# Cosine-weighted linear attention and a gated MLP on one core: load buffers shared by all batches but the second, and ten more zero matmuls in the opening

## The chip, the cores and the metric

One core of one Trainium2 chip. The metric is device time in microseconds (us) of one execution; several runs are given by their median. In the profile, PE is TensorE (matmul), PEld its weight load, DVE VectorE, ACT ScalarE, POOL GpSimd and SP SyncE; L259 is line 259 of the kernel file.

## What is computed

q, k and v have 8 batches, 8 heads, 576 positions and 64 values per head; the weights are 512 x 2048 and 2048 x 512.

```python
def phi(x, c, s):
    r = np.maximum(x, 0.0)
    return np.concatenate([r * c, r * s], axis=-1)   # cos and sin of pi/2 * pos / S
q_p, k_p = phi(q, cos_w, sin_w), phi(k, cos_w, sin_w)
kv = np.einsum('bhsf,bhsd->bhfd', k_p, v)
z = np.sum(k_p, axis=2)
num = np.einsum('bhsf,bhfd->bhsd', q_p, kv)
den = np.einsum('bhsf,bhf->bhs', q_p, z)[..., None] + 1e-06
x = (num / den)            # heads side by side: 4608 tokens x 512
h = x @ w_in
out = (h * np.cos(h)) @ w_out
```

## The kernel before

**Tiling.** A batch's 576 positions lie as 96 partitions of 6 positions (R = 6, L33). The 4608 tokens of the MLP are nine chunks of 512. Chunk c of the MLP and the attention of later batches are interleaved by hand: a chunk has 32 steps, 16 groups of the first product (M1, `m1_group`, L254: four matmuls, cosine on ScalarE, product g on VectorE) and 16 parts of the second (M2, `m2_part`, L272: four matmuls; every fourth part ends with a copy `ost` on ScalarE and stores to HBM from SP's queue). After each step, `run(c, s)` issues the attention pieces that `plan` has put there with `at(c, s, function, ...)` (L298). The order on each engine is the order of the program (`manual_schedule`, L382); the framework adds the waits, and a tile that takes a buffer over waits for the last reader of the tile before it, wherever in the program that reader stands.

**Attention pieces.** `load` (L83) is a DMA from POOL's queue that casts 32-bit inputs to 16-bit tiles k16, v16, q16. `scaled` (L100) applies the rectifier and the cosine or sine weight on VectorE, one position index i at a time (two instructions), giving kp and qp. `q_turn` (L120) transposes qp into X: on TensorE for batches 0 and 1, by a DMA transpose from SP's queue for the others (L125). `spread_v` (L159) copies v beside a column of ones (vz, whose ones are a memset on POOL, L163). `kv_head` (L171) multiplies kp and vz. `num_tile` and `normalise` (L200, L224) make the tile x of 128 tokens, which has three buffers (opool, L58). `x_turn` (L231) transposes x into XT, the input of M1: on TensorE for batches 0 and 1, by a DMA transpose from SP's queue for the others (L236).

**Where the pieces stand.** In chunk c of 1 and later: the tiles of batch c+1 at steps 16, 18, 20, 22, 24 (`plan_tiles`); for batch c+2 the q scaling and its transposes at steps 21, 23, ..., 31, v at 24, 26, 28, 30, the k scaling at 26, 28, 30 and, in chunk c+1, at 1, 3, 5 (`plan_ahead`, L349). Batch 2's q scaling ends at step 8 of chunk 1 (L342). Loads of batch 3 are issued at step 9 of chunk 1 (L345), of batch c+2 at step 1 of chunk c from chunk 2 on (L372), each as three DMAs by `loads` (L304). POOL's queue holds, in order, the loads and weight loads of the opening, the vz memsets and these loads.

**The load buffers.** lpool (L55) has two buffers for each tag, so batches take turns: 0, 2, 4, 6 in one, 1, 3, 5, 7 in the other.

**The opening** (L383 to L431): the loads are issued; TensorE multiplies a tile of zeros (`warm`, L407), 26 times 512 columns, before its first q transposes, which need qp of VectorE, which needs the q load. Then come the kp and v products of batch 0 (48 matmuls of 128 columns, L190), the first tiles, and M1 of chunk 0 in halves of 256 tokens.

Of the kernel before, what the change touches and what calls it, by code (L numbers as in the profile page):

```python
# [13 lines left out]
F16 = mybir.dt.float16  # L14
# [3 lines left out]
def kernel(  # L18
# [10 lines left out]
    B, H, S, D = q.shape  # L29
# [4 lines left out]
    PR = S // R  # L34
# [6 lines left out]
    RUN = R * D  # L41
# [10 lines left out]
    id_dr = nc.inline_tensor(np.eye(P, dtype=np.float16), name="id_const")  # L52

    cpool = ctx.enter_context(tc.tile_pool(name="cpool", bufs=1))
    lpool = ctx.enter_context(tc.tile_pool(name="lpool", bufs=2))  # L55
    apool = ctx.enter_context(tc.tile_pool(name="apool", bufs=2))
    gpool = ctx.enter_context(tc.tile_pool(name="gpool", bufs=2))
    opool = ctx.enter_context(tc.tile_pool(name="opool", bufs=3))  # L58
# [15 lines left out]
    st = {}  # L74

    def tiles_for(b):
        st[b] = dict(
            k16=lpool.tile([PR, H * RUN], F16, name="k16", tag="k16"),
            v16=lpool.tile([PR, H * RUN + D], F16, name="v16", tag="v16"),
            q16=lpool.tile([PR, H * RUN], F16, name="q16", tag="q16"),  # L80
        )

    def load(b, which, h0=0, h1=H, i0=0, i1=R):  # L83
        src = dict(k=k, v=v, q=q)[which]
        dst = st[b][which + "16"][:, 0:H * RUN]
        dst = dst.rearrange("p (h r) -> p h r", h=H)
        nc.gpsimd.dma_start(  # L87
            out=dst[:, h0:h1, i0 * D:i1 * D],
            in_=src[b].rearrange("h (p i) d -> p h (i d)", i=R)[:, h0:h1, i0 * D:i1 * D],
        )  # L90

    def load_w_in(g):
        sl = slice(g * CH, (g + 1) * CH)
        nc.gpsimd.dma_start(out=w_in_sb[:, :, sl], in_=w_in_v[:, :, sl])

    def load_w_out(g):
        sl = slice(g * 4, (g + 1) * 4)
        nc.gpsimd.dma_start(out=w_out_sb[:, sl, :], in_=w_out_v[:, sl, :])

    def scaled(b, which, i, h0=0, h1=H):  # L100
        s = st[b]
        if which + "p" not in s:
            s[which + "p"] = apool.tile([PR, R, H * F], F16, name=which + "p",
                                        tag=which + "p", bufs=1)
        dst = s[which + "p"][:, i].rearrange("p (h t d) -> p h t d", t=2, d=D)
        src = s[which + "16"][:, 0:H * RUN].rearrange("p (h i d) -> p h i d", i=R, d=D)
        for t in range(2):
            if b == 0 and (which == "k" and h0 == 4 and t == 1 or which == "q" and i == 4):
                nc.scalar.activation(
                    out=dst[:, h0:h1, t, :], in_=src[:, h0:h1, i, :], func=AF.Relu,  # L110
                    scale=CS[:, t, i:i + 1],
                )
                continue
            nc.vector.tensor_scalar(  # L114
                out=dst[:, h0:h1, t, :], in0=src[:, h0:h1, i, :],
                scalar1=0.0, scalar2=CS[:, t, i:i + 1],
                op0=ALU.max, op1=ALU.mult,
            )

    def q_turn(b, i, tag="m1"):  # L120
        s = st[b]
        if i == 0:
            s["X"] = apool.tile([P, H, S], F16, name="X", tag="X")
        if b >= 2:
            nc.sync.dma_start_transpose(  # L125
                out=s["X"][:, :, i * PR:(i + 1) * PR], in_=s["qp"][:, i],
            )
            return
        if b == 1:
            if i % 2 == 0:  # L130
                s["QT"] = psA.tile([P, 2, H, P], F16, name="QT", tag="att")
            QT = s["QT"][:, i % 2]
        elif i >= 4:
            QT = psA.tile([P, 2, H, P], F16, name="QT", tag="att")[:, 0]
        else:
            QT = psM.tile([P, H, P], F16, name="QT", tag=tag)
        for h in range(H):
            nc.tensor.matmul(  # L138
                QT[:, h, 0:PR], lhsT=s["qp"][:, i, h * F:(h + 1) * F], rhs=ID[0:PR, 0:PR],
                is_transpose=True,  # L140
            )
        if b == 1 and i % 2 == 0:
            return
        i0 = i - (b == 1)
        dst = s["X"][:, :, i0 * PR:(i + 1) * PR]
        if b == 1 and i > 1:
            nc.vector.tensor_copy(
                out=dst.rearrange("p h (a c) -> p a h c", a=2),
                in_=s["QT"][:, :, :, 0:PR],
            )  # L150
        elif b == 1:
            nc.scalar.activation(
                out=dst.rearrange("p h (a c) -> p a h c", a=2),
                in_=s["QT"][:, :, :, 0:PR], func=AF.Copy,
            )
        else:
            nc.scalar.activation(out=dst, in_=QT[:, :, 0:PR], func=AF.Copy)  # L157
# [13 lines left out]
    def kv_head(b, h):  # L171
        s = st[b]
        if h == 0 or (b == 0 and h == 4):
            s["KV"] = psA.tile([P, H, P], F32, name="KV", tag="att")
        if h == 0:
            s["kvz"] = apool.tile([P, H, D + 1], F16, name="kvz", tag="kvz")
        n = P if b == 0 else D + 1
        for i in range(R):
            if b > 0:
                nc.tensor.matmul(  # L180
                    s["KV"][:, h, 0:n], lhsT=s["kp"][:, i, h * F:(h + 1) * F],
                    rhs=s["vz"][:, h, i, 0:n], start=(i == 0), stop=(i == R - 1),
                )
                continue
            base = s["v16"][:, h * RUN + i * D: h * RUN + (i + 1) * D]
            vz = bass.AP(
                tensor=base.tensor, offset=base.offset,
                ap=[list(base.ap[0]), [H * RUN - h * RUN - i * D, 2], [1, D]],
            )
            nc.tensor.matmul(  # L190
                s["KV"][:, h], lhsT=s["kp"][:, i, h * F:(h + 1) * F], rhs=vz,
                start=(i == 0), stop=(i == R - 1),
            )
        if h % 4 == 3:
            nc.scalar.activation(  # L195
                out=s["kvz"][:, h - 3:h + 1], in_=s["KV"][:, h - 3:h + 1, 0:D + 1],
                func=AF.Copy,
            )
# [102 lines left out]
    HS = NJT  # L301
    M2S = NJT

    def loads(b, order="qkv"):  # L304
        tiles_for(b)
        for w in order:
            load(b, w)
# [70 lines left out]
    def run(c, s):  # L378
        for f, args in plan.pop((c, s), ()):
            f(*args)  # L380

    with tc.manual_schedule():  # L382
        nc.sync.dma_start(out=CS, in_=cs_dr.ap())  # L383
        nc.sync.dma_start(out=ID, in_=id_dr.ap())
        nc.vector.memset(WU, 0.0)
        nc.vector.memset(PIH, math.pi / 2.0)  # L386
        nc.scalar.activation(out=WS, in_=PIH, func=AF.Sin)
        tiles_for(0)
        load(0, "k", 0, 4)
        load(0, "k", 4, 8)  # L390
        load(0, "q", 0, H, 0, 4)
        for h in range(0, H, 2):
            load(0, "v", h, h + 2)
        nc.gpsimd.memset(st[0]["v16"][:, H * RUN:], 1.0)
        load_w_in(0)
        load(0, "q", 0, H, 4, R)
        for g in range(1, 4):
            load_w_in(g)
        load_w_out(0)
        load_w_out(1)  # L400
        loads(1, "kvq")
        load_w_out(2)
        load_w_out(3)
        loads(2, "kvq")
        W = psM.tile([P, CH], F32, name="W", tag="m2")

        def warm(n):  # L407
            for _ in range(n):
                nc.tensor.matmul(W, lhsT=WU[:, 0:P], rhs=WU, start=True, stop=True)  # L409

        warm(26)
        for h0 in (0, 4):
            for i in range(R):
                scaled(0, "k", i, h0, h0 + 4)
        for i in range(4):
            scaled(0, "q", i)
            if i < 2:
                q_turn(0, i)
        for h in range(8):
            kv_head(0, h)  # L420
        q_turn(0, 2, "m2")
        num_tile(0, 0)
        q_turn(0, 3)
        warm(1)
        num_tile(0, 1)
        warm(3)
        x_turn(0, 0)
        warm(2)
        scaled(0, "q", 4)
        x_turn(0, 1)  # L430
        num_tile(0, 2)  # L431
        for s in range(2 * HS):
            n = s // HS * (CH // 2)
            m1_group(0, s % HS, n, n + CH // 2)
            run(0, s)
        order = [(m, g) for p in (0, 2) for g in range(2) for m in (p, p + 1)]
        order += [(m, g) for m in range(NSUB) for g in range(2, 4)]
        for s, (m, g) in enumerate(order):
            m2_part(0, m, g)
            run(0, 2 * HS + s)  # L440
        for c in range(1, NCHUNK):
            for s in range(32):
                if s < NJT:
                    m1_group(c, s)
                else:
                    m2_part(c, (s - NJT) // 4, (s - NJT) % 4)
                run(c, s)
# [31 lines left out]
```

## Time and profile before

| what | us |
|---|---|
| median of 3 runs | 303.78 |
| the three runs | 304.11, 301.21, 303.78 |
| the profiled execution, its own time | 305.32 |
| its span, first to last instruction | 303.5 |
| TensorE busy | 292.9 |
| VectorE busy | 192.1 |
| ScalarE busy | 162.2 |

The profile is of one execution. Busy time is the union of an engine's instructions; idle time before a group is given with what ended it. The granted clock is the share of full speed that TensorE's throttle let through; a stretch's figure is a mean over it. The time to landing of a DMA goes from its issue to its completion. 1.8 us of the execution's own time lie outside its span.

### The profile page before, as it was taken

To read this page: it belongs to the slowest core of one execution; us is meant where nothing else is said; L and a number is where in the kernel's file an instruction comes from. 1 tells how busy PE (TensorE), PEld (TensorE's weight loads), DVE (VectorE), ACT (ScalarE), POOL (GpSimd) and SP (SyncE) were. 2 spreads that over 40 slices of the span, in tenths; PEclk is the share of its full clock that TensorE was granted. 3 is DMA by queue.
4 is the path that set the end of the run, shared out by engine and by line. 5 is a ranking of instruction groups with operands and counts; after the bars stand their busy time and mean duration, and the time that the engine had idled before them with its cause. 6 is when DMAs were issued, how large, how long until landed. Compare 5 with 4: busy or idle time off the path is not lost.

```text
span 303.5 us, 5549 instructions
## 1 busy us (share of the span) xinstructions
PE 292.9 (96%) x2088; PEld 155.1 (51%) x2088; DVE 192.1 (63%) x487; ACT 162.2 (53%) x262; POOL 29.2 (10%) x49
## 2 busy tenths in 40 slices
PE   8699999999999999999999999999999999999994
PEld 3578856554544554455445544554455444444441
DVE  2747896998579665966496739868675258107600
ACT  2559862577158715871577157725772177128521
POOL 8632103003000200020001100000000000000000
PEclk9789999999999999999999999999999999999998
DMA  7999999996996199729972997318621510121022
GB/s 103 191 206 205 205 205 202 229 191 102 193 192 153 33 181 232 137 59 170 212 163 63 160 188 183 81 38 147 141 49 38 129 53 2 35 69 38 0 69 69
DMA packets 73515, 38.81 MB, mean 128 GB/s; under 512 B 46352, under 2 KB 68880, under 8 KB 73488
## 3 DMA queue, kind: packets, MB, share of 16 engines
q0 software_dynamic: 23888, 18.35, 40.5%
q1 hardware_dynamic: 49600, 20.10, 33.7%
q8 instruction: 16, 0.26, 0.3%
q14 instruction: 11, 0.09, 0.1%
HBM read 36.74 MB, written 9.44 MB: 152 GB/s over the span
## 4 chain that ended last, share of the span: by engine, by line
PE 79%; DMA 9%; DVE 7%; ACT 2%; issue 1%; POOL 0%; ACTq 0%; DVEq 0%; POOLq 0%
PE M L259 35%; PE M L278 34%; DMA XT<-x 6%; PE KV L180 4%; DVE g L268 3%; PE NP L206 3%; DMA q<-in_q_dram 3%; DVE qp L114 2%; PE KV L190 2%; PE QT L138 1%; DVE kp L114 1%; ACT co L265 1%; DVE x L226 1%; PE XP L244 1%; POOL k L87 0%
## 5 line engine op out<-in xcount | busy, mean ns | idle before, releaser
L278 PE MATMUL M<-w_out_sb,g 128*128 128x512 f16 x576 | 132.3, 379 | 0.1
L259 PE MATMUL M<-XT,w_in_sb 128*128 128x512 f16 (+1 forms) x640 | 129.8, 358 | 1.7 <-DVE g L268 1.3
L268 DVE TENSOR_TENSOR g<-M,co 128x512 f16<-128x512 f32 (+1 forms) x160 | 98.6, 633 | 47.2 <-ACT co L265 47.0
L265 ACT ACTIVATE co<-M,PIH 128x512 f32<-128x512 f32 (+1 forms) x160 | 101.9, 646 | 28.7 <-PE M L259 25.3
L259 PEld LDWEIGHTS <-w_in_sb 128*128 128x128 f16 x640 | 61.2, 98 | 61.1 <-issue 2.5
L278 PEld LDWEIGHTS <-g 128*128 128x128 f16 x576 | 53.7, 98 | 58.7 <-issue 0.3
L285 ACT ACTIVATE ost<-M 128x512 f32<-128x512 f32 x36 | 21.5, 597 | 91.0 <-PE M L278 85.2
L226 DVE TENSOR_TENSOR x<-NP,rd 128x512 f16<-128x512 f32 (+1 forms) x42 | 27.9, 665 | 18.4 <-DMA XT<-x 17.3
L114 DVE TENSOR_SCALAR kp<-k,CS 96x512 f16<-96x512 f16 (+1 forms) x102 | 29.0, 346 | 4.8 <-DMA k<-in_k_dram 4.8
L114 DVE TENSOR_SCALAR qp<-q,CS 96x512 f16<-96x512 f16 x94 | 28.5, 350 | 0.4 <-DMA q<-in_q_dram 0.4
L206 PEld LDWEIGHTS <-X 128*128 128x128 f16 x320 | 15.3, 98 | 8.4 <-ACT X L157 0.4
L167 ACT ACTIVATE vz<-v 96x768 f16<-96x768 f16 x24 | 18.7, 830 | 0.0
L213 DVE TENSOR_SCALAR dn<-NP 128x8 f32<-128x8 f32 x40 | 6.4, 161 | 18.3 <-PE NP L206 18.2
L206 PE MATMUL NP<-kvz,X 128*128 128x65 f16 x320 | 16.9, 194 | 0.1
L163 POOL MEMSET vz<- 96x96 f16 x7 | 1.3, 186 | 147.6 <-PE KV L180 147.6
L180 PEld LDWEIGHTS <-kp 96*128 96x128 f16 x336 | 12.5, 98 | 3.1
L180 PE MATMUL KV<-vz,kp 96*128 96x65 f16 x336 | 13.0, 193 | 0.0
L409 PE MATMUL W<-WU 128*128 128x512 f16 x32 | 9.2, 440 | 1.2 <-DVE PIH L386 1.2
L195 ACT ACTIVATE kvz<-KV 128x260 f16<-128x260 f32 x16 | 6.2, 387 | 6.8 <-PE KV L190 3.9
L217 DVE RECIPROCAL rd<-dn 128x8 f32<-128x8 f32 x40 | 8.1, 203 | 1.4
L138 PE MATMUL QT<-ID,qp 96*128 96x96 f16 x96 | 6.3, 220 | 2.6 <-DVE qp L114 2.6
L87 POOL DMA_DIRECT2D v<-in_v_dram x11 | 7.9, 722 | 3.4 <-DMA w_in_sb<-in_moe_w_in_dram 1.7
(27 smaller groups left out, 67.3 us busy)
## 6 DMA issues: line engine op xcount, KB each, us to landing
out_dram<-ost SPq DMA_DIRECT2D x24, 192.0 KB, 2.5
k<-in_k_dram POOLq DMA_DIRECT2D x7, 576.0 KB, 9.5
v<-in_v_dram POOLq DMA_DIRECT2D x7, 576.0 KB, 13.3
q<-in_q_dram POOLq DMA_DIRECT2D x7, 576.0 KB, 7.3
out_dram<-ost SPq DMA_DIRECT2D x24, 128.0 KB, 2.4
w_in_sb<-in_moe_w_in_dram POOLq DMA_DIRECT2D x4, 512.0 KB, 11.8
w_out_sb<-in_moe_w_out_dram POOLq DMA_DIRECT2D x4, 512.0 KB, 19.1
out_dram<-ost SPq DMA_DIRECT2D x24, 64.0 KB, 2.0
```

The costliest lines, as they stand in the source:

```text
L114: nc.vector.tensor_scalar(out=dst[:, h0:h1, t, :], in0=src[:, h0:h1, i, :], scalar1=0.0, scalar2=CS[:, t, i:i + 1], op0=ALU.max, op1=ALU.mult,
L138: nc.tensor.matmul(QT[:, h, 0:PR], lhsT=s["qp"][:, i, h * F:(h + 1) * F], rhs=ID[0:PR, 0:PR], is_transpose=True,)
L167: nc.scalar.activation(out=dst, in_=src[:, h:h + 2], func=AF.Copy)
L180: nc.tensor.matmul(s["KV"][:, h, 0:n], lhsT=s["kp"][:, i, h * F:(h + 1) * F], rhs=s["vz"][:, h, i, 0:n], start=(i == 0), stop=(i == R - 1),)
L206: nc.tensor.matmul(NP[:, h // 4, o:o + D + 1], lhsT=s["X"][:, h, c0:c0 + P], rhs=s["kvz"][:, h], start=True, stop=True,)
L226: nc.vector.tensor_tensor(out=x4[:, a0:a1], in0=np4[:, a0:a1, :, 0:D], in1=rd[:, a0:a1].broadcast_to((P, a1 - a0, 4, D)), op=ALU.mult,)
L259: nc.tensor.matmul(M1[:, n0:n1], lhsT=w_in_sb[:, i, j * P:(j + 1) * P], rhs=XT[:, i, c * CH + n0:c * CH + n1], start=(i == 0), stop=(i == ...
L265: nc.scalar.activation(out=co[:, n0:n1], in_=M1[:, n0:n1], func=AF.Sin, bias=PIH, scale=1.0,)
L268: nc.vector.tensor_tensor(out=st["g", c][:, j, n0:n1], in0=M1[:, n0:n1], in1=co[:, n0:n1], op=ALU.mult,)
L278: nc.tensor.matmul(M2, lhsT=st["g", c][:, j, m * P:(m + 1) * P], rhs=w_out_sb[:, j], start=(j == 0), stop=(j == NJT - 1),)
L285: nc.scalar.activation(out=ost, in_=M2, func=AF.Copy)
L409: nc.tensor.matmul(W, lhsT=WU[:, 0:P], rhs=WU, start=True, stop=True)
```

## The change

One buffer for each of k16, v16 and q16, with a tag of their own for batch 1; so batches 0, 2, 3, 4, 5, 6 and 7 share one set and batch 1 has another. The number of tiles in memory is as before. The loads of batches 3 to 7 are issued in the order q, v, k instead of q, k, v; batches 1 and 2 keep their own order, k, v, q. The opening has 36 zero matmuls where there were 26.

```diff
-    lpool = ctx.enter_context(tc.tile_pool(name="lpool", bufs=2))
+    lpool = ctx.enter_context(tc.tile_pool(name="lpool", bufs=1))
...
     def tiles_for(b):
+        odd = "o" if b == 1 else ""
         st[b] = dict(
-            k16=lpool.tile([PR, H * RUN], F16, name="k16", tag="k16"),
-            v16=lpool.tile([PR, H * RUN + D], F16, name="v16", tag="v16"),
-            q16=lpool.tile([PR, H * RUN], F16, name="q16", tag="q16"),
+            k16=lpool.tile([PR, H * RUN], F16, name="k16", tag="k16" + odd),
+            v16=lpool.tile([PR, H * RUN + D], F16, name="v16", tag="v16" + odd),
+            q16=lpool.tile([PR, H * RUN], F16, name="q16", tag="q16" + odd),
         )
...
-    def loads(b, order="qkv"):
+    def loads(b, order="qvk"):
         tiles_for(b)
         for w in order:
             load(b, w)
...
-        warm(26)
+        warm(36)
```

## The prediction

> **What bounds the kernel now.** I read the page first, then TensorE by stretch, then the stretches where it is not full.
>
> ```profile
> span 303.5 us, 5549 instructions
> ...
> PE 292.9 (96%) x2088; PEld 155.1 (51%) x2088; DVE 192.1 (63%) x487; ACT 162.2 (53%) x262; POOL 29.2 (10%) x49
> ...
> PEclk9789999999999999999999999999999999999998
> ```
>
> TensorE is busy for 292.9 of 303.5 us, so only two things can move the end: the 10.6 us in which it is idle, and how fast it is clocked while busy. The clock row has one dip near the start. The busy time by stretch resolves it (columns: PE, PEld, DVE, ACT, POOL busy, then the granted clock):
>
> ```profile
> 4.50:8.60 4.10, 4.10 (x19) 1.66 (x17) 2.68 (x11) 1.24 (x4) 3.91 (x7) 1.00 1.31 178
> 8.60:11.10 2.50, 0.00 (x1) 0.00 (x0) 2.09 (x11) 1.26 (x4) 0.35 (x1) 1.00 1.28 184
> 11.10:11.90 0.80, 0.70 (x8) 0.49 (x8) 0.80 (x4) 0.00 (x0) 0.80 (x2) 0.65 1.29 195
> 11.90:12.50 0.60, 0.60 (x8) 0.60 (x9) 0.60 (x2) 0.60 (x1) 0.57 (x2) 0.50 1.30 209
> 17.50:18.50 1.00, 1.00 (x21) 1.00 (x19) 0.00 (x0) 0.46 (x2) 0.66 (x1) 0.67 1.24 205
> ```
>
> After 4.1 us of zero matmuls TensorE idles 2.5 us, and the clock then falls to half: 0.65 over 0.80 us means a fall at 11.34, 0.67 over the last one a rise at 18.16, so 6.8 us at half clock. What runs in them, by the timeline of TensorE (start, length, line, count):
>
> ```profile
> 11.16 1.56 PE L138 MATMUL QT<-ID,qp 96*128 96x96 f16 x16 [2.56 <-DVE qp L114]
> 12.52 5.32 PE L190 MATMUL KV<-v,kp 96*128 96x128 f16 x48
> 17.64 0.76 PE L138 MATMUL QT<-ID,qp 96*128 96x96 f16 x8
> ```
>
> From 59 to 244 us TensorE is full but for two places. The waits of TensorE between 120 and 215 us (total, times, longest), then the chain of waits around the first place:
>
> ```profile
> PE M L259 <- DVE g L268: 1.1, 2, 0.5
> ```
> ```profile
> 140.19 9.70 DMA XT<-x
> ...
> 149.98 0.69 DVE x L226
> ```
>
> VectorE waits for a DMA transpose that took 9.70 us, holding one of the three x buffers; everything behind it on VectorE is late, the first g of the next chunk too, and TensorE waits for that g. The DMA issues by stretch say when a transpose is slow (count, median us to landing), 120.5 to 152 and 183 to 213.3 us:
>
> ```profile
> XT<-x SPq DMA_TRANSPOSE x5, 7.2
> ```
> ```profile
> XT<-x SPq DMA_TRANSPOSE x6, 2.4
> ```
>
> The first stretch has a load of q, k and v in it, the second none. The timeline of POOL shows the loads starting at a chunk's thirteenth group:
>
> ```profile
> 47.76 0.77 POOL L87 DMA_DIRECT2D q<-in_q_dram  x1 [0.38 <-issue]
> 71.20 0.77 POOL L87 DMA_DIRECT2D q<-in_q_dram  x1 [3.70 <-DVE qp L114]
> 104.41 0.77 POOL L87 DMA_DIRECT2D q<-in_q_dram  x1 [0.37 <-DVE g L268]
> 134.85 0.77 POOL L87 DMA_DIRECT2D q<-in_q_dram  x1 [0.35 <-DVE g L268]
> ```
>
> **The change, part one: ten zero matmuls.** The first eight zero matmuls start 0.43 us apart and seventeen of the rest take 3.55 us, 0.21 each. Ten more add 2.1 us: TensorE ends its zeros at 8.60 + 2.13 = 10.73, before the first q transpose at 11.16, which waits for VectorE's qp. They hide whole behind that wait (2.56 us, of which 0.43 stays); if the cover were gone, at most 2.1 us would show. What they change is that TensorE is busy from 4.5 to 10.7, so I take it that the clock is not lowered at 11.34. Priced at full clock by nearest rows: eight q transposes 0.34 (sixteen take 0.68 at 45.6 us); the second eight can't start before 11.90 (their qp) and end at 12.24; 48 KV matmuls of 128 columns go by the x transposes (L244, 128 columns, four in 0.22), 0.055 each, 2.6 us; so KV ends at 14.9 instead of 17.84. The other bound is the 65-column KV (24 in 0.76, 0.032 each): 1.5 us. No gain at all is the bound on the other side. I take 128 columns for 128 columns. What is late next? v: its four parts land at 3.51+7.7, 4.14+7.9, 4.77+7.9 and 5.39+8.1 = 11.2, 12.0, 12.7, 13.5; the pairs of heads start at 12.2, 12.9, 13.6, 14.2, none late. From KV's end to the first M1 matmul (21.95) lies a chain of ScalarE and VectorE pieces, 4.1 us at full clock already, so M1 starts at 19.0. Its weights: groups land at 16.0, 19.6, 22.4, 24.9; needed at 19.0, 21.3, 23.4, 25.6. Batch 1: k lands at 33.1, v 35.9, q 39.0; needed at 40.2, 39.7, 43.4 less 2.9. All met, the last weight group by 0.7, v by 0.9. **Minus 2.9 us.**
>
> [...]
>
> **Part two: the buffers.** Batches 0, 2, 3, ... share one set, batch 1 has its own. Loads of batches 0, 1 and 2 had these very buffers apart already and stay. Load 3 took batch 1's buffers at 47.76; now it needs batch 2's, whose last reader is the sixth q scaling, the one that released the load at 71.20. So load 3 goes where load 4 was. Load 4 needs batch 3's: q is last read at about 91.4 (step 31 of chunk 1), v at step 30, k by the sixth k scaling, 97.2 (step 5 of chunk 2). So loads 4 to 7 run in the first 10 to 15 us of chunks 2 to 5 instead of beside the XT transposes of chunks 1 to 4; load 3 takes load 4's place in chunk 1. Issues stay 15, 0.77 us each, in the same order on POOL.
>
> New waits on POOL: q of load 3 for 23.4 us, behind it v, k and the ones of vz (batch 3), which ScalarE needs at 83.5 us. k of loads 4 to 7 for about 5 us, behind it only the next vz memset, not needed until step 24, some 17 us later. Both at nothing. Arrival: load 4 of before, in the same stretch, landed first, second and third after 7.3, 9.5 and 12.6 us: 78.5, 81.5, 85.3. Batch 3's first uses stand at 81.2 (q), 83.5 (v), 88.2 (k); in the new order each has 2 us or more. That is what the order q, v, k costs or saves: nothing.
>
> SP's queue is passed: around 89 to 105 us it issues the last XT transpose, up to six X transposes and two pairs of output stores. These now meet a load: X from 2.6 to at most 7.5 us landing (its range here). Last X issued 97.6, landed 105.1 at worst, its reader at step 22, about 112. The last XT serves a chunk further on. The output buffer is next written at step 19. Nothing.
>
> The gain: XT transposes in chunks 2, 3, 4 fall from 7.2 to 7.8 us towards 2.4; VectorE's waits there (17.3 us in all, 3.0 in chunk 1 which stay) go, and TensorE's 1.1 us with them. Where does it stall next? In chunks 5 and 6, without loads, it doesn't. Bounds: 0 (the waits move to where the loads go) to 1.3 (all L259 waits). **Minus 1.1 us.**
>
> [...]
>
> **Sum.** The profiled execution took 305.32 us (span 303.5 and 1.8 around it). 305.32 - 2.9 - 1.1 = 301.3. It stands 1.5 above the median of 303.78; the same 4.0 off the median gives **299.8**.
>
> **Rivals.**
> (a) The clock brings nothing: it falls anyway, or the timed runs mostly do not have the dip. For: 301.21 beside 304.11 among three runs, a distance of the dip's size. Against: two of three runs and the profile are at the slow end. Then only part two counts: 303.78 - 1.1 = 302.7. If the slow first matmuls last 16 instead of 8, the zeros end at 12.3 and the KV starts 0.7 later: 303.4.
> (b) Contention only moves. For: the loads meet SP's late transposes at 89 to 105 us. Against: their readers have 7 us. 303.78 - 2.9 = 300.9.
> (c) Slower: load 3 comes late. Issued 23 us later than before, it has 2.7 us to its first use on VectorE; loads in this trace took up to 22.2 us to land. 71.2 + 22.2 = 93.4 is 12.2 after the use at 81.2; VectorE has taken a wait of 5 us in a chunk at a cost of 0.5, so some 4.5 are free and 7.7 reach TensorE: 303.78 - 2.9 + 7.7 = 308.6. It decides from a landing at about 88.6 (3 us past the slack) for no gain. Against: the 22.2 came in a full queue at 30 us, in this stretch the trace has 7.3.
>
> **How the numbers follow.** Forecast 0.60, (a) 0.21, (b) 0.12, (c) 0.07. The range: the low end has KV at the 65-column price, 1.1 us less than forecast, 298.7; the high end is (a)'s 303.4; it leaves out (c). The forecast's own range is 298.7 to 300.7. Over 1% faster means below 300.74, about what a measurement of this kernel can tell from no change: the forecast and a sixth of (b), 0.62; within 1%: (a) and the rest of (b), 0.31; slower 0.07.
>
> **What would show it.** Right: granted clock 1.00 from 11 to 18 us; 48 KV matmuls in 2.6 us; first M1 matmul near 19.0; 0.4 us idle before the first q transpose; loads at about 68, 88, 119 us; XT landing near 2.4 us in chunks 2 to 4; no TensorE wait for g after 60 us. Wrong: a clock of 0.50 after the zeros; VectorE or ScalarE waiting for batch 3's load near 79 to 85 us; TensorE waiting in chunk 1; KV waiting for v.

## The result and the profile after

The changed kernel takes 301.39 us (median of 21 runs, 300.48 to 302.99); the kernel before, on the same chips, 303.78 (21 runs, 301.21 to 305.28). The ratio is 0.9936, interval 0.9913 to 0.9959: 2.4 us less by the medians and 1.9 by the means, where the prediction had 4.0. The profiled execution took 300.48, its span is 298.7, and it lies at the fast end of the 21, as the profile of before lies at the slow end of its own. From the page:

```profile
span 298.7 us, 5575 instructions
...
PE 291.7 (98%) x2098; PEld 153.3 (51%) x2098; DVE 192.9 (65%) x487; ACT 162.1 (54%) x262; POOL 31.1 (10%) x49
...
PEclk9999999999999999999999999999999999999999
```

Of the 4.8 us between the two spans, 1.2 are busy time of TensorE, though it runs ten matmuls more; the rest is idle time that is gone. The dip of the clock row is gone as well. The opening in the timeline of TensorE (start, length, line, count):

```profile
1.20 9.91 PE L410 MATMUL W<-WU 128*128 128x512 f16 x36 [1.20 <-DVE PIH L387]
10.95 0.84 PE L139 MATMUL QT<-ID,qp 96*128 96x96 f16 x16
11.62 2.84 PE L191 MATMUL KV<-v,kp 96*128 96x128 f16 x48
...
18.50 1.03 PE L260 MATMUL M<-XT,w_in_sb 128*128 128x256 f16 x8 [0.35 <-DVE dn L214]
```

48 KV matmuls take 2.84 us where they took 5.32, and the first M1 matmul starts at 18.50 where it started at 21.95. The 0.4 us of idle time that were to be left before the first q transpose are not there: TensorE goes from the zeros to the transposes without a wait. The waits of TensorE (total, times, longest) have no transpose and no late g of chunks 3 and 4 in them (all of them lie before 55 us):

```profile
PE W L410 <- DVE PIH L387: 1.2, 1, 1.2
PE XP L245 <- DVE x L227: 0.5, 2, 0.3
PE M L260 <- DVE dn L214: 0.4, 1, 0.4
PE M L260 <- DVE g L269: 0.2, 1, 0.2
```

The loads stand where the prediction put them (68 and 88 us; the third, forecast at 119, is 2.8 us earlier); the timeline of POOL:

```profile
67.75 0.77 POOL L88 DMA_DIRECT2D q<-in_q_dram  x1 [23.82 <-DVE qp L115]
88.94 0.77 POOL L88 DMA_DIRECT2D q<-in_q_dram  x1 [18.70 <-DVE qp L115]
94.89 0.78 POOL L88 DMA_DIRECT2D k<-in_k_dram  x1 [4.42 <-DVE g L269]
116.20 0.77 POOL L88 DMA_DIRECT2D q<-in_q_dram  x1 [15.63 <-DVE qp L115]
```

One thing differs from what was written. These are the DMA issues between 117 and 148 us (count, median us to landing):

```profile
X<-qp SPq DMA_TRANSPOSE x7, 8.4
XT<-x SPq DMA_TRANSPOSE x5, 2.4
```

XT lands in 2.4 us as forecast, but X now takes 8.4, and over the whole execution up to 14.5, against 7.5 before. So this pair of profiles agrees with both mechanisms and even shows 4.8 us; the timed runs don't. A single execution is not the median, and the experiments had to say how it differs.

### The profile page after: what moved, and what is told of

Same layout as the page of the kernel before. It is cut to its first block, busy times and chain, and to the rows that moved or that the text cites. A ratio compares the mean times of both kernels' runs of the same rounds, so it can differ in the third digit from the quotient of the medians.

```text
span 298.7 us, 5575 instructions
## 1 busy us (share of the span) xinstructions
PE 291.7 (98%) x2098; PEld 153.3 (51%) x2098; DVE 192.9 (65%) x487; ACT 162.1 (54%) x262; POOL 31.1 (10%) x49
## 4 chain that ended last, share of the span: by engine, by line
PE 93%; DVE 4%; ACT 1%; issue 0%; ACTq 0%
PE M L279 42%; PE M L260 38%; PE W L410 4%; PE KV L181 4%; PE NP L207 3%; DVE g L269 3%; PE QT L139 1%; ACT co L266 1%; PE KV L191 1%; PE XP L245 1%; DVE x L227 0%; ACT ost L286 0%; DVE qp L115 0%; DVE XT L251 0%; DVE rd L218 0%
## 5 line engine op out<-in xcount | busy, mean ns | idle before, releaser
L115 DVE TENSOR_SCALAR qp<-q,CS 96x512 f16<-96x512 f16 x94 | 27.8, 343 | 0.1
L88 POOL DMA_DIRECT2D q<-in_q_dram x9 | 7.0, 775 | 91.1 <-DVE qp L115 89.1
L410 PE MATMUL W<-WU 128*128 128x512 f16 x42 | 11.7, 436 | 1.2 <-DVE PIH L387 1.2
L88 POOL DMA_DIRECT2D k<-in_k_dram x9 | 6.9, 771 | 27.8 <-DVE kp L115 20.4
```

The lines of the kernel that those rows point to most:

```text
L88: nc.gpsimd.dma_start(out=dst[:, h0:h1, i0 * D:i1 * D], in_=src[b].rearrange("h (p i) d -> p h (i d)", i=R)[:, h0:h1, i0 * D:i1 * D],)
L115: nc.vector.tensor_scalar(out=dst[:, h0:h1, t, :], in0=src[:, h0:h1, i, :], scalar1=0.0, scalar2=CS[:, t, i:i + 1], op0=ALU.max, op1=ALU.mult,
```

## The experiments

Ratios are to the kernel before on the same chip, as recorded. Means are of all timed executions of one kernel on one chip, so a quotient of two means can differ from the ratio beside it (0.994 and 0.9924 for e2). "Body" is the time from the first M1 matmul to the end of the span, worked out from a profile.

### The kernel before, for its clock (e1)

No edit. 

> The kernel before once more, for the granted clock of its timed executions. Theory 1 (the dip of the clock is there in only part of the executions): the executions fall into two groups, those with a mean granted clock of about 0.985 to 0.990 (6.8 us at half clock cost 0.011 of it) and those at 0.996 or more, and the first are 2.9 us longer on average; the first are a third to a half of all. Theory 2 (the dip is nearly always there and the buffers lose what the zeros gain): nearly all at 0.990 or less. Ratio to the kernel before 1.000 either way.

Measured: 1.0006 (0.9974 to 1.0038). The 45 executions of this kernel on that chip fall into three groups by their mean granted clock, not two: 11 at 0.996 or more with a mean of 301.9 us, 16 between with 303.3, 18 at 0.989 or less with 304.6. This profile is of the middle group. By stretch of time (TensorE's, then the other engines' busy time, the granted clock third from the end):

```profile
11.90:12.50 0.60, 0.41 (x10) 0.41 (x11) 0.60 (x2) 0.60 (x1) 0.60 (x2) 1.00 1.28 206
12.50:13.50 1.00, 1.00 (x16) 1.00 (x13) 1.00 (x4) 0.95 (x2) 1.00 (x2) 0.64 1.24 206
13.50:14.50 1.00, 1.00 (x13) 1.00 (x11) 0.10 (x1) 0.00 (x0) 1.00 (x2) 0.50 1.30 204
15.50:16.50 1.00, 1.00 (x15) 1.00 (x13) 0.00 (x0) 0.00 (x0) 0.00 (x0) 0.66 1.40 202
```

0.64 puts the fall at 12.78 and 0.66 the rise at 16.18: half clock for 3.4 us, half of the 6.8 in the first profile. (The mean granted clock also holds a fall at the very end, 0.86 after 296 us in the first profile, so the groups are read from it only roughly.) So one execution in four has no dip, the others have a short or a long one, which cost about 1.4 and 2.7 us. Theory 1 (the dip is not always there) holds, with a larger share than it gave.

### The ten zero matmuls alone (e2)

```diff
-        warm(26)
+        warm(36)
```

> The ten zero matmuls alone. Theory 1: no execution under 0.99 of the clock; the mean falls by a third to a half of 2.9 us, ratio 0.995 to 0.997; a profile without the dip, the first M1 matmul at 18.5 to 19.0, and still 1.1 us of TensorE waiting for g in chunks 3 and 4. Theory 2: ratio 0.990 to 0.991.

Measured: 0.9924 (0.9901 to 0.9947), mean 301.67 against 303.5 of the kernel before, no execution under 0.996 of the clock. The interval reaches Theory 2's ratio and not Theory 1's; the difference of the means, 1.8 us, lies between the two. The clock settles it: e1 speaks against Theory 2's dip in nearly all, and here the dip is gone in all twelve where it was there in three of four. The first M1 matmul stands at 19.30. But with the old buffers this profiled execution has no wait for g in chunks 3 and 4 at all: the stall of 1.1 us that the prediction priced is not in every execution either (1.1 in the first profile, 0.3 in e1's, none here).

### The buffers and the load order alone (e3)

The lines of the diff without the last. 

> The shared buffers and the order q, v, k alone, 26 zero matmuls. Theory 1: 1.1 us less in each execution, ratio 0.996 to 0.997, the clock's two groups as in the kernel before; no TensorE wait for g after 60 us. Theory 2: about 1 us more, ratio 1.003.

Measured: 0.9980 (0.9947 to 1.0013), half a microsecond less in the mean (302.99 against 303.5), not to be told from nothing. The dip is there as before (9 of 12 under 0.996). There is no wait for g after 60 us, but e2's profile, with the old buffers, had none either, so this doesn't show that the buffers took the stall away. Theory 2's 1.003 lies outside the interval; Theory 1's 0.996 to 0.997 lies inside, though the mean has half its size.

### Both, again (e4)

No edit to the changed kernel. 

> The changed kernel once more, beside its parts on the same chip. Theory 1: ratio 0.992 to 0.995, the product of the two parts within their intervals. Theory 2: the same ratio, but as a product of 0.990 and 1.003.

Measured: 0.9943 (0.9913 to 0.9973), mean 301.64. Beside 301.67 for the zeros alone, the buffers add nothing that can be told from zero (-0.03 +- 0.48 us, 2.1 standard errors). The ratio is inside Theory 1's range, but the product of the two parts would be 0.990, just outside the interval; Theory 2's second factor fell in e3. The profiled execution was the slowest of the ten, 302.70, and shows most of the reason; the waits of TensorE after 90 us, the timeline of TensorE, and the landing of the X transpose that was issued at 97.71 us:

```profile
PE NP L207 <- DMA X<-qp: 1.3, 1, 1.3
```
```profile
110.84 0.43 PE L207 MATMUL NP<-kvz,X 128*128 128x65 f16 x8 [1.28 <-DMA X<-qp]
```
```profile
X<-qp SPq DMA_TRANSPOSE x1, 13.1
```

97.71 + 13.1 = 110.8: the fourth tile's matmuls start as that transpose lands, 1.28 us late. The body is 281.6 us; in the first profile of the changed kernel it was 280.2. That is 1.4 of the 2.2 us between the two executions; the other 0.8 is the opening, whose first M1 matmul starts at 19.26 here and at 18.50 there.

### k first, so that the loads begin after most X transposes (e5)

The changed kernel, with

```diff
-    def loads(b, order="qvk"):
+    def loads(b, order="kqv"):
```

> The changed kernel with the loads of batches 3 to 7 in the order k, q, v, so that k's wait for the sixth k scaling (step 5 of the next chunk) holds q and v back too, and the loads begin some 6 us later, after most X transposes. Theory 1 (the load has moved onto the X transposes of SP's queue, whose longest landing rose from 7.5 to 14.5 us, and TensorE now and then waits for X): longest X landing under 10 us, no TensorE wait for X or g after 60 us, XT landing still near 2.4 us; ratio 0.990 to 0.992, some 0.5 us less than the changed kernel. Theory 2 (the X transposes have room enough; what is missing was never there): the same time as the changed kernel, ratio 0.993 to 0.995.

Measured: 0.9912 (0.9882 to 0.9942), mean 300.88, all twelve within 0.9 us. Longest X landing 9.1, body 280.2, no wait for X. That is what Theory 1 gave.

### No loads of batches 3 to 7 (e6, and again as g2)

```diff
         tiles_for(b)
...
+        if b > 2:
+            st[b] = {n: st[2][n] for n in ("k16", "v16", "q16")}
+            return
```

(the added lines stand first in `loads`)

> The changed kernel without the loads of batches 3 to 7, which are computed from batch 2's tiles: the most that any placing of these loads can bring. Theory 1: from the first M1 matmul to the end 280.2 us, as in the best profiled executions, every time; ratio 0.989 to 0.991, about 0.6 to 1.2 us less than the changed kernel. Theory 2: no less than the changed kernel, ratio 0.993 to 0.995, and the executions still lie 2 us apart because of the opening.

Measured: 0.9922 (0.9892 to 0.9953), mean 300.96, body 280.2. The kernel leaves out these loads and so computes something else; as a floor for any placing of them it is 300.96, and k first is at it (-0.08 +- 0.25 us). Beside the changed kernel on other chips (301.55 to 301.64) about 0.6 us were lost to the loads, as Theory 1 has it.

### Fewer and more zeros (e7, e8)

The changed kernel with `warm(31)`, and with `warm(46)`.

> The changed kernel with 31 zero matmuls; the idle time before the first q transpose is about 1.5 us instead of 2.5 (26) or 0.4 (36). If the dip comes from the idle share of a stretch of time: rarer or shorter dips than with 26, in 0 to 30 per cent of the executions, ratio 0.993 to 0.996. If any idle time of over 1 us brings it: as often as with 26 (three in four), ratio 0.997 to 0.999.

> The changed kernel with 46 zero matmuls, which end at about 12.7 us instead of 10.6, so the q transposes start 1.2 to 1.6 us later than their input. No dip; the end 0.8 to 1.4 us later than with 36 if the opening stays on TensorE's path, ratio 0.996 to 0.999; the same as with 36 if the weights or the loads set the start of M1.

Measured for 31: 0.9922 (0.9889 to 0.9956), mean 300.92, no execution under 0.996, though TensorE idles 1.48 us before the first transpose in its profile. So idle time of over 1 us doesn't always bring the dip; the first reading fits, though the time is somewhat below its range; whether the idle share is the cause is not shown. For 46: 1.0008 (0.9973 to 1.0043), mean 303.66 beside 300.88 of e5 on the same chip, with no dip. Its timeline of TensorE:

```profile
1.20 12.23 PE L410 MATMUL W<-WU 128*128 128x512 f16 x46 [1.20 <-DVE PIH L387]
13.27 0.84 PE L139 MATMUL QT<-ID,qp 96*128 96x96 f16 x16
```

The zeros now end after their cover. M1 starts at 20.82, 2.1 us later than in e5's profile (18.73) and 1.4 to 2.3 later than in the ten profiles with 36 zeros. This profiled execution (304.14) is 3.4 us longer than e5's (300.71); the rest of that is a body of 281.6, with 0.5 us of waiting for X and 0.3 for g (the order of the loads differs too). So the opening does lie on the path, and either expectation for 46 was too mild.

### Zeros against order, on one chip (f1 to f4)

| kernel | ratio, interval | mean us, against f1 |
|---|---|---|
| f1: 36, q v k (the changed kernel) | 0.9957, 0.9928 to 0.9986 | 301.62 |
| f2: 36, k q v | 0.9922, 0.9892 to 0.9951 | 300.96, -0.66 +- 0.53 |
| f3: 31, q v k | 0.9917, 0.9889 to 0.9945 | 300.96, -0.65 +- 0.50 |
| f4: 31, k q v | 0.9911, 0.9878 to 0.9944 | 300.79, -0.82 +- 0.47 |

(+- is 2.1 standard errors of the difference of the two means.)

> The changed kernel (36 zeros, order q, v, k), as the corner that the next three are compared with on one chip. 301.4 to 301.6 us on average, the timed executions 1.5 to 2.5 us apart.

> 36 zeros, order k, q, v. Theory 1 (two small costs side by side: X transposes that land late, and zeros that end after q is ready in part of the executions): 0.3 to 0.5 us less than 36 with q, v, k on average. Theory 2 (only the late X transposes): 0.6 us less. Theory 3 (only the overshooting zeros): the same as 36 with q, v, k.

> 31 zeros, order q, v, k. Theory 1: 0.3 to 0.5 us less than 36 with q, v, k. Theory 2: the same. Theory 3: 0.6 us less. No dip of the clock.

> 31 zeros, order k, q, v: the version that should beat both kernels. Theory 1: the fastest of the four, 0.6 to 1.0 us less than 36 with q, v, k, ratio to the kernel before 0.989 to 0.991. Theory 2: as 36 with k, q, v. Theory 3: as 31 with q, v, k.

Either edit brings back two thirds of a microsecond, both together hardly more. Theories 2 and 3 each name one cause and fall on the other's edit. Theory 1 adds two costs up; its sizes lie inside the errors of all three, though not at their centres. f4 is the fastest version measured, 0.8 us under the changed kernel; against f2 and f3 the difference is within the errors. The DMA issues of f2 in the stretch shown above for the changed kernel:

```profile
X<-qp SPq DMA_TRANSPOSE x7, 2.6
XT<-x SPq DMA_TRANSPOSE x6, 2.5
```

Both transposes are quick at once when the loads start at a chunk's step 5.

### What the overshoot costs by itself, and two more profiles (g1 to g4)

g1 is e6 with `warm(31)`, g2 is e6, g3 and g4 are the changed kernel.

> 31 zeros, without the loads of batches 3 to 7, which are computed from batch 2's tiles. If the overshoot of 36 zeros costs by itself: 0.3 to 0.6 us less than 36 without loads, 300.4 to 300.7 us on average. If it costs only together with the late X transposes: the same as 36 without loads, 300.9.

> 36 zeros, without those loads, beside it on the same chip: 300.9 to 301.0 us on average, the executions within 1 us of each other.

> The changed kernel, one look. If late X transposes make its slow executions: at 302 us or more TensorE waits 1 us or more for X in chunks 2 to 5, at 301.5 or less it waits 0.3 or less. If the opening makes them: the first M1 matmul is late by as much as the execution, 280.2 us from it to the end.

> The same as the look before it, in another execution: slow with a wait for X, or slow with a late first M1 matmul.

Measured: g1 0.9930 (0.9901 to 0.9959), mean 300.99; g2 0.9939 (0.9912 to 0.9966), mean 301.09. Without loads the five zeros cost 0.10 +- 0.19 us, so an overshoot by itself is not the 0.65, and Theory 1's two costs side by side are not shown either. The two profiled executions of the changed kernel took 300.78 and 301.13, both with a body of 280.2 to 280.3 and no wait for X. Of five profiled executions of the changed kernel, the four between 300.48 and 301.45 have the body of 280.2 and no such wait, and the one at 302.70 has 1.3 us of it. Among the four the time follows the opening one for one: M1 starts at 18.50, 18.78, 19.14 and 19.46, and they take 300.48, 300.78, 301.13 and 301.45. So a microsecond of the spread is the opening. What lies above it fits late X transposes; with one such execution among the profiles that isn't shown. Why 31 zeros spare it, though X still takes up to 14.2 us to land there (f3), stays open.

## Why the prediction missed

The step from the zeros to the clock was right (of 12 executions each, 9 of e1 with 26 zeros and none of e2 with 36 lie under 0.996), and so was the gain of XT's transposes (2.4 us to landing between 117 and 148 us; 7.2 between 120.5 and 152 before). Three steps failed: "Minus 2.9 us" measured 1.8, "Minus 1.1 us" measured nothing on top of it (-0.03 +- 0.48), and the step of SP's queue, costed at nothing, was not nothing.

**"Minus 2.9 us."** Most steps hold: the ten zeros remove most of the idle time and the dip with it, KV takes 2.84 us where 2.6 was forecast (0.059 each, not 0.055), M1 moves to about 19 (18.50 to 19.46 in the ten profiles with 36 zeros). "They hide whole behind that wait" doesn't: in these ten profiles the slow start of the zeros, 0.43 us apart, covers not always eight of them but 6 to 13, so the 36 end between 10.49 and 11.83 us instead of at 10.73. In eight of the ten no wait is left before the q transposes. But above all the price is that of the longest dip. Priced by executions it is 2.7 us in 18 of 45, 1.4 in 16 and nothing in 11, 1.6 us on average; the zeros alone measured 1.8 +- 0.5 in the mean. The three runs shown had said so (301.21 beside 304.11), and rival (a) quoted them, but as a case of its own instead of as a mixture that lowers the forecast.

**"Minus 1.1 us."** The waits of VectorE for XT go as described, 17.3 us to 3.7, and XT lands in 2.4. But the stall of TensorE that they had caused is 0 to 1.1 us by execution, and the execution that was priced had the most of it.

**"X from 2.6 to at most 7.5 us landing (its range here)... Nothing."** This is the step whose mechanism failed. The range came from 36 X transposes of which 29 ran beside no load of q, k or v (2.6 to 4.7 us), and was carried to a place where 22 of 36 have one beside them: up to 14.5 us. The margin shrank from the other side too. With the opening shorter, the reader at step 22 moved from 112.09 to 108.64 in the first profile, while the last X issue moved only from 97.57 to 97.04, since SP's queue is itself slower there (two X issues take 4.76 us where they took 2.54). In e4 the reader was due at 109.56 and X landed at 110.8. With k first, which takes the load off X, 0.66 +- 0.53 us come back. Rival (b), contention only moves, was right about the place.

**The sum** was taken off the median, 303.78, with both terms priced from one execution at the slow end (305.32): that subtracts what the median execution has less of. The mean fell from 303.49 to 301.55, by 1.9 us, which the zeros alone account for.

Rival (c) didn't occur: load 3 landed 7.8 (q), 10.5 (v) and 13.5 us (k) after its issue, and nobody waited for it. Gaps of 2.04 us in e1, 2.13 in e3 and 2.56 in the first profile each came before half clock, while none of 39 executions with 31 zeros fell under 0.996; the four of them that were profiled had gaps of 0, 0.60, 1.32 and 1.48 us. No execution with 26 zeros and without the dip was profiled, so whether its gap is shorter, or the same at another moment, stays open. With one set of buffers the loads still ran beside TensorE's work (no engine waited for one after 55 us in the first profile of the changed kernel), and the kernel was no slower (e3, 0.9980). On contention, of the 36 X transposes in that profile the 22 beside a load of q, k or v took 2.6 to 14.5 us to land and the other 14 took 2.6 to 4.5; what the two share is not shown.

## What to carry to other kernels

A profile shows one execution: before a dip or a stall in it is priced in full, look at the spread of the timed runs, and give the term the share of executions that have it. When a transfer is moved off one neighbour, price the new neighbour by rows that had the same company, not by the range over all rows. Keep TensorE's filler just inside the wait that covers it: five fewer kept the whole gain here (0.9917 in f3), ten more lost it (1.0008 in e8), and the end of the zeros moved by more than a microsecond from one profile to the next (10.49 to 11.83 us).

## What the runs showed of the hardware

The half clock came in pieces of 3.4 us (e1) and 6.8 us (the first profile), in executions of one unchanged kernel; on the four chips of the experiments 35 of 128 executions of the kernel before show none (a mean granted clock of 0.996 or more). And a DMA transpose of an unchanged size took 2.5 to 4.7 us without the loads (X in e6) and up to 15.4 (e7) with them.
